# Second feed-forward layer: the output drain on VectorE alone, a longer planned transfer, an earlier planned load

## The chip, the cores and the metric

The kernel runs on one core of one Trainium2 chip. The metric is device time in microseconds for one execution, the median of several runs; a profile of one further execution is at hand. Engines are named as in the profile: PE is TensorE, PEld its weight loads, DVE is VectorE, ACT is ScalarE, POOL is GpSimd, SP is the queue that issues most DMA transfers.

## The reference

A block-causal attention over 4 sequences of 576 tokens (8 heads of 64), then two feed-forward layers on the 2304 x 512 result. The second layer, which the change touches, is this:

```python
def _moe2_ref(x, w_in, w_out, alpha):       # x 2304x512, w_in 512x2048, w_out 2048x512
    h = x @ w_in
    g = np.maximum(h, 0.0) + alpha * np.minimum(h, 0.0)
    return (g @ w_out).astype(np.float32)
```

Every operand of the second layer's matmuls is split into a high and a low fp16 part, and each product is three matmuls (high by high, high by low, low by high; helper `three`, L1030).

## The kernel before

**Tiles and steps.** The second layer works on nine tiles of 256 tokens, n = 0 to 8, and for each on eight steps s = 0 to 7 of 256 of the 2048 hidden columns. Tiles 0 and 1 run together, interleaved step by step; from tile 2 on the tiles follow one another. A step has three parts. `up2` (PE) makes h in one PSUM bank by 24 matmuls of 256 columns; its banks rotate through the tags h, h, acc, acc. `act2` applies the PReLU and splits: DVE makes u (L1199 twice, then L1203), from tile 3 on POOL adds four sums (L1211), ACT copies to the high fp16 half of g (L325, the line of the helper `act`), DVE subtracts to get the low half (L1224). `down2` (PE) multiplies g by the second weights into the tile's accumulators. For tiles 0 to 2 (`down_plain`) there are two accumulator banks of 512 columns and 12 matmuls of 512 columns per step. From tile 3 on the output block is built from seven products (Strassen's scheme, `factor`), M1 to M7 in slots 0 to 6 of the program's list, which lie in half banks of four PSUM banks with the tags e, e, s, o: 21 matmuls of 256 columns per step. PE takes them in the order of slots 0, 5 (first e bank), 3, 4 (second e bank), 2, 1 (s), 6 (o).

**The overlap of tiles.** PE runs the ups some three steps ahead of the downs. The last downs of tile n-1 stand between the first ups of tile n, and after down (n-1, step 7) PE runs up (n, step 4) and up (n, step 5) back to back before down (n, step 0). That down writes the same e banks that tile n-1 has just filled, so tile n-1's accumulators have to be drained in the time of these two ups.

**The drain.** `store_plain` (tiles 0 to 2) scales two banks of 512 columns into the SBUF tile `osb`, the first on ACT, the second on DVE (L1271). `store2` (tile 3 on) copies slot 0 on ACT into one quarter of `osb`, then DVE adds the other slots, scaled by +1 or -1 times the tile's factor, in seven instructions (L1319) that write quarter by quarter; the ACT copy's result is the operand of the first of them. Two output transfers follow.

**The next x and its scale.** `load2(n)` fetches tile n's x from DRAM into `xs` (one buffer, four transfers, L1131), takes the greatest absolute value of each partition (DVE, L1136, into `xsc`), and for n of 2 and more sends these 128 values out to DRAM and back to all partitions (`row`, then `rows`, both L317, the line of the helper `dma`), where DVE takes the greatest (L1146). A few tiny DVE instructions (L454, L1151) make the scale, and ACT and DVE split x into the fp16 pair `xh` (ACT L325, DVE L1157), which `up2` reads; `xh` has two buffers. `load2(n + 1)` is called in the loop over steps, at s = 1 of tile n.

**Who sets the order.** All instructions are first listed with a due time `plan.at`; `Plan.order` then simulates the engines with written-in costs and gives each engine one fixed order: among the instructions that are ready when the engine is free, the one with the smallest due time. On the chip each engine runs its list strictly in order. A transfer's planned cost comes from the size that is passed to `dma`; the third argument is in KiB, and `extra = kib / 350` us is added to its planned end:

```python
def dma(dst, src, kib, reads=(), writes=(), after=()):
    return add("DMA", 0.5, lambda: nc.sync.dma_start(dst(), src()), reads, writes, kib / 350.0, after)
```

The size passed does not alter the transfer. `rows` was given 64 KiB, which plans 0.18 us beyond the fixed planned part.

Of the kernel before, what the change touches and what calls it, by code (L numbers as in the profile page):

```python
# [14 lines left out]
ALU = mybir.AluOpType  # L15
# [217 lines left out]
def dve2_cost(n, pointers=0, shared=False):  # L233
    return (155 + 60 * pointers + n / 0.96) * (1.1 if shared else 1.0) * 1e-3
# [15 lines left out]
def block_causal_attention_silu_prelu(  # L250
# [65 lines left out]
    def dma(dst, src, kib, reads=(), writes=(), after=()):  # L316
        return add("DMA", 0.5, lambda: nc.sync.dma_start(dst(), src()), reads, writes, kib / 350.0, after)  # L317

    def act(n, dst, src, func, reads, writes, psum=False, **kw):
        pointers = sum(callable(kw.get(x)) for x in ("scale", "bias"))  # L320
        cost = act_cost(n, psum, pointers, "accum_out" in kw)

        def fn():
            k = {x: y() if callable(y) else y for x, y in kw.items()}
            nc.scalar.activation(dst(), src(), func, **k)  # L325

        return add("ACT", cost, fn, reads, writes)
# [799 lines left out]
    def load2(n, after=()):  # L1127
        s = sb(ff2_p, [128, T2 // 32, KD, 32], F32, "xs")
        x2 = x2d[places[n]]
        for z in range(4):  # L1130
            add("DMA", 0.5, lambda z=z: nc.sync.dma_start(  # L1131
                s()[32 * z:32 * z + 32].rearrange("p i k t -> p i (k t)"),
                x2()[:, 128 * z:128 * z + 128].rearrange("(i p) n -> p i n", p=32)),
                [x2], [(s, z)], extra=T2 / 350.0, after=after)
        sc = xsc[n] = sb(ff2_p, [128, 4], F32, "xsc", 3)
        add("DVE", dve_cost(KD * T2), lambda: nc.vector.tensor_reduce(  # L1136
            sc()[:, 0:1], s().rearrange("p i k t -> p (i k t)"), axis=AX.X, op=ALU.max, apply_absolute_value=True),
            [s], [sc])
        if n < TOGETHER2:
            spread(lambda: sc()[:, 0:1], [sc], lambda: sc()[:, 1:2], [sc])  # L1140
        else:
            row = sb(dram_p, [1, 128], F32, f"row{n}")
            rows = sb(ff2_p, [128, 128], F32, "rows")
            dma(lambda: row().rearrange("o p -> p o"), lambda: sc()[:, 0:1], 1, [sc], [row])
            dma(lambda: rows(), lambda: row().to_broadcast([128, 128]), 64, [row], [rows])
            add("DVE", dve_cost(128), lambda: nc.vector.tensor_reduce(sc()[:, 1:2], rows(), axis=AX.X, op=ALU.max),  # L1146
                [rows], [sc])
        m = lambda: sc()[:, 1:2].bitcast(I32)
        tiny(m, m, 0x7F800000, None, ALU.bitwise_and, None, sc)
        tiny(m, m, float(27 << 23), float(TOP << 23), ALU.max, ALU.subtract, sc)  # L1150
        add("DVE", dve_cost(6), lambda: nc.vector.reciprocal(sc()[:, 2:3], sc()[:, 1:2]), [sc], [sc])  # L1151
        t = sb(ff2_p, [128, 2, KD, T2], F16, "xh2", 2)
        for kk in range(KD):
            part = lambda e, kk=kk: t()[:, e, kk].rearrange("p (i t) -> p i t", t=32)
            act(T2, lambda part=part: part(0), lambda kk=kk: s()[:, :, kk], AF.Copy, [s, sc], [(t, (0, kk))],
                scale=lambda: sc()[:, 2:3])
            add("DVE", dve_cost(T2, 1, 1), lambda part=part, kk=kk: nc.vector.scalar_tensor_tensor(  # L1157
                part(1), s()[:, :, kk], sc()[:, 2:3], part(0), op0=ALU.mult, op1=ALU.subtract),
                [s, sc, (t, (0, kk))], [(t, (1, kk))])
        for kind in "io":  # L1160
            if kind in wsc:
                add("DVE", dve_cost(1, 1, 1), lambda kind=kind: nc.vector.tensor_scalar(
                    sc()[:, 1:2], sc()[:, 1:2], wsc[kind]()[:, 2:3], 2.0**(G_EXP if kind == "i" else 0),
                    op0=ALU.mult, op1=ALU.mult), [sc, wsc[kind]], [sc])
        tiny(lambda: sc()[:, 3:4], lambda: sc()[:, 1:2], -1.0, None, ALU.mult, None, sc)
        xh2[n] = t
# [99 lines left out]
    def store_plain(n):  # L1266
        sc = xsc[n]
        e = sb(ff2_p, [128, 2, DM], F32, "osb", 2)
        for t, a in enumerate(acc.pop(n)):
            if t:  # L1270
                add("DVE", dve2_cost(DM, 1), lambda a=a: nc.vector.tensor_scalar(  # L1271
                    e()[:, 1], a(), sc()[:, 1:2], None, op0=ALU.mult), [a, sc], [(e, t)])
            else:
                act(DM, lambda: e()[:, 0], lambda a=a: a(), AF.Copy, [a, sc], [(e, t)], psum=True,
                    scale=lambda: sc()[:, 1:2])
            row = 0
            for r0, count in rows_of(2 * places[n] + t):
                dma(lambda r0=r0, count=count: out[r0:r0 + count],
                    lambda row=row, count=count, t=t: e()[row:row + count, t], count * 2, [(e, t)])
                row += count  # L1280
# [18 lines left out]
    def store2(n):  # L1299
        if n < PLAIN:  # L1300
            return store_plain(n)
        sc = xsc.pop(n)
        banks = acc.pop(n)
        e = sb(ff2_p, [128, 2, DM], F32, "osb", 2)
        c11, c12, c21, c22 = ((j, half) for j in range(2) for half in range(2))
        at = lambda c: lambda: e()[:, c[0], 256 * c[1]:256 * c[1] + 256]

        def part(i):
            bank, half = SLOTS_OF[i]
            return (banks[bank], half), lambda: banks[bank]()[:, 256 * half:256 * half + 256]  # L1310

        key, m1 = part(0)
        act(256, at(c11), m1, AF.Copy, [key, sc], [(e, c11)], psum=True, scale=lambda: sc()[:, 1:2])
        for i, col, base, dst in (
            (5, 1, c11, c22), (3, 3, c22, c21), (4, 1, c22, c12), (4, 1, c21, c22), (2, 1, c11, c11), (1, 3, c21, c21),
            (6, 3, c12, c12),
        ):
            key, m = part(i)
            add("DVE", dve2_cost(256, 1), lambda m=m, col=col, base=base, dst=dst: nc.vector.scalar_tensor_tensor(  # L1319
                at(dst)(), m(), sc()[:, col:col + 1], at(base)(), op0=ALU.mult, op1=ALU.add),  # L1320
                [key, sc, (e, base)], [(e, dst)])
            for j in range(2):
                if i != {0: 6, 1: 1}[j]:
                    continue
                row = 0
                for r0, count in rows_of(2 * places[n] + 1 - j):
                    dma(lambda r0=r0, count=count: out[r0:r0 + count],
                        lambda row=row, count=count, j=j: e()[row:row + count, j], count * 2,
                        [(e, c) for c in ((c11, c12), (c21, c22))[j]])
                    row += count  # L1330
# [115 lines left out]
    for s in range(half + 1):  # L1446
        base = total + 1 + STEP_FIRST * s
        if s < half:
            for m in order2[2 * s:2 * s + 2]:
                plan.at = base - 1.0  # L1450
                load_w(1, "o", m, scanned)
                plan.at = base
                split_w(1, "o", m)
            for n in range(TOGETHER2):
                plan.at = base + 0.4 * n
                up2(n, s)
                act2(n, s)
            if s == 3:
                load2(TOGETHER2, after=stores[-2:])
        elif low_parts:  # L1460
            low_parts.pop()(())
        if s:
            for n in range(TOGETHER2):
                plan.at = base + FIRST_DOWN + 0.4 * n
                down2(n, s - 1)
    for n in range(TOGETHER2):
        store2(n)
    for k in range((N2 - TOGETHER2) * half + 1):
        n, s = divmod(k, half)
        n += TOGETHER2  # L1470
        base = after_first + STEP2 * k
        if n < N2:
            plan.at = base
            up2(n, s)
            act2(n, s)
            if n == TOGETHER2:
                plan.at = base + 1.0
                mix_o(s)
            if s == 1 and n + 1 < N2:
                load2(n + 1)  # L1480
        elif low_parts:
            low_parts.pop()(())
        if k >= 1:
            pn, s = divmod(k - 1, half)
            plan.at = base + DOWN2 + (SWITCH - 0.4 * s if s < 3 else 0.0)
            down2(pn + TOGETHER2, s)
            if s == half - 1:
                store2(pn + TOGETHER2)

    with tc.manual_schedule():  # L1490
# [86 lines left out]
```

## Time and profile before

| | |
|---|---|
| median of 3 runs | 913.66 us (913.22 to 916.06) |
| the profiled execution | 913.75 us, span 912.0 us |
| PE busy | 885.8 us, 97% of the span |
| DVE busy | 694.3 us, 76% |
| ACT busy | 465.2 us, 51% |
| POOL busy | 263.5 us, 29% |
| mean granted PE clock | 0.996 of full speed |

The span is the time from the first to the last recorded instruction. The second layer's work on PE takes the time from about 529 us to the end. An engine's busy time counts instructions alone; the end of a matmul is modelled, so consecutive matmuls overlap a little in the rows, and the time that a stretch of PE work takes is read from the start of its first matmul to the start of the next piece.

### The profile page before, as it was taken

The numbers are of one execution on the slowest core, as the hardware profiler recorded it, in microseconds if no ns is written. First come the engines' busy times: TensorE is split into PE (matmuls) and PEld (weight loads), VectorE is DVE, ScalarE is ACT, GpSimd is POOL, SyncE is SP. The second block draws the span as 40 slices with busy tenths as digits, with TensorE's granted clock in tenths as the row PEclk, the third lists the DMA queues.
The fourth block names the chain that finished last, engine by engine and source line by source line (L and its number), as shares of the span: only waits on it lengthen the run. The fifth ranks groups of instructions, "written<-read, shape, count | busy, mean of one in ns | idle before, by whom it ended". The sixth has DMA issues, their size and how long they took to land. (4 is left out here: it accounts for less than half of the span.)

```text
span 912.0 us, 18221 instructions
## 1 busy us (share of the span) xinstructions
PE 885.8 (97%) x6845; PEld 741.3 (81%) x6845; DVE 694.3 (76%) x1557; ACT 465.2 (51%) x1070; POOL 263.5 (29%) x380
## 2 busy tenths in 40 slices
PE   7899999999999999999999999999989999999997
PEld 5688888898988888889788786667658888888886
DVE  5999767688888888887489897896575856757673
ACT  6987556677868777775236753342122222213121
POOL 6501002232212222221000000572044544536552
PEclk9999999999999999999999999999999999999999
DMA  9952134487665766659698981441110110100010
GB/s 316 407 215 53 35 94 110 110 145 151 123 162 119 155 134 130 151 134 251 222 327 321 268 282 42 142 160 47 27 50 4 47 28 24 28 28 1 24 24 24
DMA packets 134248, 116.55 MB, mean 128 GB/s; under 512 B 100240, under 2 KB 111504, under 8 KB 134160
## 3 DMA queue, kind: packets, MB, share of 16 engines
q1 hardware_dynamic: 133008, 111.19, 44.4%
q0 software_dynamic: 1152, 4.19, 1.1%
q8 instruction: 54, 0.88, 0.5%
q14 instruction: 34, 0.28, 0.1%
HBM read 78.65 MB, written 14.16 MB: 102 GB/s over the span
## 5 line engine op out<-in xcount | busy, mean ns | idle before, releaser
L1030 PE MATMUL h<-x_all,w0i 128*128 128x256 f32 (+1 forms) x1440 | 224.7, 308 | 2.4 <-ACT x_all L325 1.5
L1030 PEld LDWEIGHTS h<-x_all,w0i 128*128 128x128 f32 x1440 | 199.8, 191 | 22.9 <-issue 3.8
L1030 PEld LDWEIGHTS <-w1i 128*128 128x128 f16 x1728 | 168.9, 98 | 24.7 <-issue 0.5
L325 ACT ACTIVATE g<-u 128x896 f16<-128x896 f32 (+1 forms) x72 | 60.7, 843 | 223.6 <-POOL u L1211 112.0
L1030 PEld LDWEIGHTS <-g 128*128 128x128 f16 x1296 | 127.2, 98 | 51.9 <-issue 8.5
L1030 PE MATMUL acc<-w0o,g 128*128 128x512 f32 x672 | 168.8, 394 | 0.2
L1211 POOL TENSOR_TENSOR u<-u 128x128 f32<-128x128 f32 x192 | 116.6, 628 | 162.9 <-DVE u L1203 75.6
L1030 PEld LDWEIGHTS acc<-w0o,g 128*128 128x128 f32 x672 | 122.4, 188 | 27.5 <-issue 2.5
L1030 PE MATMUL acc<-xh,w1i 128*128 128x256 f16 x864 | 100.0, 273 | 0.0
L335 POOL TENSOR_TENSOR g<-t,g 128x512 fp32r<-128x512 f32 x40 | 53.0, 1326 | 161.7 <-ACT g L325 157.7
L1030 PE MATMUL h<-xh,w1i 128*128 128x256 f16 x864 | 99.4, 273 | 0.0
L1224 DVE SCALAR_TENSOR_TENSOR g<-u,g 128x896 f16<-128x896 f32 (+1 forms) x72 | 74.1, 1030 | 12.7 <-ACT g L325 12.6
L325 ACT ACTIVATE p<-p,stat 128x512 f16<-128x512 f32 (+2 forms) x112 | 63.3, 608 | 22.0 <-issue 7.7
L1030 PE MATMUL e<-w1op,g 128*128 128x512 f16 (+1 forms) x336 | 67.6, 333 | 3.9 <-ACT osb L325 2.6
L325 ACT ACTIVATE p<-e,stat 128x256 f32<-128x256 f32 (+2 forms) x98 | 51.0, 527 | 33.2 <-DVE stat L946 22.3
L325 ACT ACTIVATE t<-h 128x512 f32<-128x512 f32 x72 | 43.0, 597 | 44.4 <-PE h L1030 37.7
L1030 PE MATMUL e<-w1om,g 128*128 128x256 f16 x432 | 56.6, 275 | 4.8 <-DVE osb L1319 4.2
L1075 DVE SCALAR_TENSOR_TENSOR t<-t,h 128x512 f32<-128x512 f32 x72 | 49.0, 680 | 13.7 <-ACT t L325 12.5
L325 ACT ACTIVATE g<-t 128x512 fp32r<-128x512 f32 x72 | 45.4, 630 | 19.5 <-DVE t L1075 19.0
L885 DVE SCALAR_TENSOR_TENSOR p<-p,stat,p 128x384 f16<-128x384 f32 (+1 forms) x64 | 48.4, 796 | 4.4 <-ACT p L325 4.1
L1030 PE MATMUL e<-w0o,g 128*128 128x512 f32 x192 | 49.4, 393 | 0.0
L416 POOL DMA_DIRECT2D kept<-wso x8 | 4.8, 602 | 136.2 <-DVE wso L371 70.3
(167 smaller groups left out, 1336.1 us busy)
## 6 DMA issues: line engine op xcount, KB each, us to landing
st<-qkv_b SPq DMA_DIRECT2D x16, 800.0 KB, 4.8
raw0i<-w_in SPq DMA_DIRECT2D x16, 512.0 KB, 9.9
raw0o<-w_out SPq DMA_DIRECT2D x16, 512.0 KB, 9.9
scano<-w_out SPq DMA_DIRECT2D x16, 512.0 KB, 6.6
raw1i<-w_in SPq DMA_DIRECT2D x16, 512.0 KB, 5.3
raw1o<-w_out SPq DMA_DIRECT2D x16, 512.0 KB, 5.9
scani<-w_in SPq DMA_DIRECT2D x13, 512.0 KB, 4.4
x<-x2e SPq DMA_DIRECT2D x18, 256.0 KB, 2.4
```

The costliest lines, as they stand in the source:

```text
L325: nc.scalar.activation(dst(), src(), func, **k)
L335: eng.tensor_tensor(lo(), src(), hi().bitcast(F32), op=ALU.subtract)
L416: add("POOL", 1.5, lambda: nc.gpsimd.dma_start(kept[s](), both().rearrange("p c n -> p (c n)")), [a, b], [kept[s]])
L885: add("DVE", dve_cost(n, 1, 1), lambda hl=hl, rr=rr, pr=pr: nc.vector.scalar_tensor_tensor(hl()[:, :, 1], pr(), rr(), hl()[:, :, 0], op0=A ...
L1030: nc.tensor.matmul(dst, lhs(a), rhs(b), start=(start and n == 0), stop=(stop and n == 2))
L1075: add("DVE", dve_cost(2 * T1), lambda: nc.vector.scalar_tensor_tensor(t(), t(), 1.0, h3(), op0=ALU.add, op1=ALU.mult), [t, h], [t])
L1211: add("POOL", pool2_cost(128, 2.5), lambda out_=out_, x=x, y=y, op=op: nc.gpsimd.tensor_tensor(u()[:, out_], u()[:, x], u()[:, y], op=op), ...
L1224: add("DVE", dve2_cost(blocks * 128, 0, True), lambda: nc.vector.scalar_tensor_tensor(side(1)(), src(), 2.0**-G_EXP, side(0)(), op0=ALU.mu ...
```

## The change

In `store_plain` and `store2` the ACT copy becomes a DVE `tensor_scalar`, so that a tile's whole drain is on DVE. The due times of the drains are set earlier (by 8.0 for tiles 0 and 1, by 5.0 for the others). The planned size of `rows` goes from 64 to 2600 KiB, which plans it to land 7.43 us after the fixed part instead of 0.18. `load2(n + 1)` is called at s = 0 instead of s = 1.

```diff
-            dma(lambda: rows(), lambda: row().to_broadcast([128, 128]), 64, [row], [rows])
+            dma(lambda: rows(), lambda: row().to_broadcast([128, 128]), 2600, [row], [rows])
...
         for t, a in enumerate(acc.pop(n)):
-            if t:
-                add("DVE", dve2_cost(DM, 1), lambda a=a: nc.vector.tensor_scalar(
-                    e()[:, 1], a(), sc()[:, 1:2], None, op0=ALU.mult), [a, sc], [(e, t)])
-            else:
-                act(DM, lambda: e()[:, 0], lambda a=a: a(), AF.Copy, [a, sc], [(e, t)], psum=True,
-                    scale=lambda: sc()[:, 1:2])
+            add("DVE", dve2_cost(DM, 1), lambda a=a, t=t: nc.vector.tensor_scalar(
+                e()[:, t], a(), sc()[:, 1:2], None, op0=ALU.mult), [a, sc], [(e, t)])
...
         key, m1 = part(0)
-        act(256, at(c11), m1, AF.Copy, [key, sc], [(e, c11)], psum=True, scale=lambda: sc()[:, 1:2])
+        add("DVE", dve2_cost(256, 1), lambda: nc.vector.tensor_scalar(
+            at(c11)(), m1(), sc()[:, 1:2], None, op0=ALU.mult), [key, sc], [(e, c11)])
...
+    plan.at -= 8.0
     for n in range(TOGETHER2):
         store2(n)
...
-            if s == 1 and n + 1 < N2:
+            if s == 0 and n + 1 < N2:
                 load2(n + 1)
...
             if s == half - 1:
+                plan.at -= 5.0
                 store2(pn + TOGETHER2)
```

On PE the order is row for row the same before and after. On DVE and ACT it moves from the point where tile 2's `rows` is read onward; all changed places lie in the second layer.

The first place is DVE at the end of tile 3, while PE is in tile 4. `g_9165` and `g_9222` are g of tile 4's steps 1 and 2; the u rows are those of step 3. Before:

```order
L1199 TENSOR_SCALAR u<-acc,alpha_sb 128x256 x2
L1203 SCALAR_TENSOR_TENSOR u<-acc,u 128x512
L1319 SCALAR_TENSOR_TENSOR osb<-e,xsc,osb 128x256
L1224 SCALAR_TENSOR_TENSOR g_9222<-u,g_9222 128x896
L1319 SCALAR_TENSOR_TENSOR osb<-e,xsc,osb 128x256 x2
L1319 SCALAR_TENSOR_TENSOR osb<-s,xsc,osb 128x256
L1319 SCALAR_TENSOR_TENSOR osb<-e,xsc,osb 128x256
L1319 SCALAR_TENSOR_TENSOR osb<-o,xsc,osb 128x256
```

And the same place in the change:

```order
L1199 TENSOR_SCALAR u<-acc,alpha_sb 128x256
L1309 TENSOR_SCALAR osb<-e,xsc 128x256
L1199 TENSOR_SCALAR u<-acc,alpha_sb 128x256
L1316 SCALAR_TENSOR_TENSOR osb<-e,xsc,osb 128x256
L1203 SCALAR_TENSOR_TENSOR u<-acc,u 128x512
L1316 SCALAR_TENSOR_TENSOR osb<-e,xsc,osb 128x256 x2
L1316 SCALAR_TENSOR_TENSOR osb<-s,xsc,osb 128x256
L1316 SCALAR_TENSOR_TENSOR osb<-e,xsc,osb 128x256
L1316 SCALAR_TENSOR_TENSOR osb<-o,xsc,osb 128x256
L1316 SCALAR_TENSOR_TENSOR osb<-s,xsc,osb 128x256
L1224 SCALAR_TENSOR_TENSOR g_9222<-u,g_9222 128x896
```

The drain has eight DVE instructions instead of seven, it begins between the two u instructions of step 3, and g of step 2 stands behind it instead of behind its first instruction.

The second place is DVE at the end of tiles 0 and 1, where tile 3's x is measured (L1136) and its scale comes back (L1146). `g_8268` and `g_8290` are g of tile 2's steps 1 and 2. Before:

```order
L1271 TENSOR_SCALAR osb<-e,xsc 128x512
L1224 SCALAR_TENSOR_TENSOR g_8268<-u,g_8268 128x512
L1136 TENSOR_REDUCE xsc<-xs 128x1
L1271 TENSOR_SCALAR osb<-o,xsc 128x512
L1199 TENSOR_SCALAR u<-acc,alpha_sb 128x256 x2
L1203 SCALAR_TENSOR_TENSOR u<-acc,u 128x512
L1224 SCALAR_TENSOR_TENSOR g_8290<-u,g_8290 128x512
L1199 TENSOR_SCALAR u<-h,alpha_sb 128x256
L1146 TENSOR_REDUCE xsc<-rows 128x1
```

The change has there (the gap holds u and g of tile 2's steps 4 and 5, three rows a step):

```order
L1270 TENSOR_SCALAR osb<-e,xsc 128x512 x2
L1224 SCALAR_TENSOR_TENSOR g_8268<-u,g_8268 128x512
L1270 TENSOR_SCALAR osb<-s,xsc 128x512
L1270 TENSOR_SCALAR osb<-o,xsc 128x512
L1136 TENSOR_REDUCE xsc<-xs 128x1
L1199 TENSOR_SCALAR u<-acc,alpha_sb 128x256 x2
L1203 SCALAR_TENSOR_TENSOR u<-acc,u 128x512
...
L1199 TENSOR_SCALAR u<-acc,alpha_sb 128x256 x2
L1203 SCALAR_TENSOR_TENSOR u<-acc,u 128x512
L1146 TENSOR_REDUCE xsc<-rows 128x1
```

All four drains stand ahead of L1136 now, and between L1136 and L1146 there are four steps' u work instead of one and a half.

The third place is SP's queue there: the transfers of tile 2's x scale are done, `x_3` and `x_4` are the x of tiles 3 and 4.

```order
 L1131 DMA xs<-x_3_3530 32x8x128 x4
-L317 DMA out<-osb 128x512 x3
-L317 DMA row_8322<-xsc 128x1
-L317 DMA out<-osb 128x512
-L317 DMA rows<-row_8322 128x128
+L317 DMA out<-osb 128x512 x4
+L317 DMA row_8344<-xsc 128x1
+L317 DMA rows<-row_8344 128x128
 L1131 DMA xs<-x_4_4538 32x8x128 x4
```

`row` stands behind four output transfers instead of three; the loads of `xs` keep their place behind the previous tile's `rows`.

## Rows read from the trace of the kernel before

**Rows 1.** PE's waits, 560 to 912 us: us in total, times, longest.

```profile
PE e L1030 <- DVE osb L1319: 4.2, 4, 1.5
PE e L1030 <- ACT osb L325: 2.6, 1, 2.6
PE e L1030 <- DVE g L1224: 1.3, 1, 1.3
PE e L1030 <- DVE osb L1271: 0.5, 1, 0.5
```

**Rows 2.** Stretches of PE work: bounds, length, busy us (instructions), granted clock, DMA.

```profile
662.31:664.90 2.59, 2.59 (x14) 1.00 0.07 23
667.52:671.58 4.06, 2.76 (x14) 1.00 0.02 5
628.43:633.67 5.24, 5.24 (x50) 1.00 0.48 155
671.58:679.63 8.05, 5.41 (x50) 1.00 0.22 65
883.52:885.81 2.29, 2.29 (x23) 1.00 0.61 140
679.63:683.94 4.31, 3.77 (x21) 0.60 0.34 122
720.95:723.84 2.89, 2.58 (x24) 1.00 0.19 72
760.84:764.78 3.94, 2.58 (x23) 1.00 0.16 56
801.79:805.43 3.64, 2.58 (x23) 1.00 0.15 56
842.44:846.51 4.07, 2.58 (x23) 1.00 0.14 51
```

**Rows 3.** PE in order of time, tile 5's first down: start, us, work [idle<-releaser].

```profile
763.02 0.81 PE L1030 MATMUL e<-w1om,g 128*128 128x256 f16 x6 [1.36 <-DVE osb L1319]
...
764.78 2.78 PE L1030 MATMUL acc<-xh,w1i 128*128 128x256 f16 x24
```

**Rows 4.** ACT in order of time, at the ends of tiles 2 and 4.

```profile
678.91 0.67 ACT L325 ACTIVATE osb<-e,xsc 128x512 f32<-128x512 f32 x1
...
759.34 0.46 ACT L325 ACTIVATE osb<-e,xsc 128x256 f32<-128x256 f32 x1
```

**Rows 5.** DVE in order of time, at the ends of tiles 2 and 4.

```profile
680.33 0.74 DVE L1271 TENSOR_SCALAR osb<-e,xsc 128x512 f32<-128x512 f32 x1
...
759.83 0.48 DVE L1319 SCALAR_TENSOR_TENSOR osb<-e,xsc,osb 128x256 f32<-128x256 f32 x1 [1.35 <-ACT osb L325]
760.23 1.17 DVE L1224 SCALAR_TENSOR_TENSOR g<-u,g 128x896 f16<-128x896 f32 x1
761.32 0.86 DVE L1319 SCALAR_TENSOR_TENSOR osb<-e,xsc,osb 128x256 f32<-128x256 f32 x2
...
762.50 0.47 DVE L1319 SCALAR_TENSOR_TENSOR osb<-e,xsc,osb 128x256 f32<-128x256 f32 x1
```

**Rows 6.** DVE's waits, whole span.

```profile
DVE xsc L1146 <- DMA rows<-row: 54.4, 7, 9.9
```

**Rows 7.** DVE in order of time, x of tiles 3 and 4.

```profile
628.07 1.21 DVE L1136 TENSOR_REDUCE xsc<-xs 128x1 f32<-128x1024 f32 x1
...
642.26 0.29 DVE L1146 TENSOR_REDUCE xsc<-rows 128x1 f32<-128x128 f32 x1 [9.62 <-DMA rows<-row]
...
645.95 1.66 DVE L1157 SCALAR_TENSOR_TENSOR xh<-xs,xsc,xh 128x256 f16<-128x256 f32 x4
...
665.46 0.29 DVE L1146 TENSOR_REDUCE xsc<-rows 128x1 f32<-128x128 f32 x1 [9.94 <-DMA rows<-row]
```

**Rows 8.** SP in order of time, tile 3's scale on its way out.

```profile
629.31 0.33 SPq L317 DMA_DIRECT2D row<-xsc  x1
```

**Rows 9.** PE in order of time, tile 3's first up.

```profile
649.27 2.78 PE L1030 MATMUL h<-xh,w1i 128*128 128x256 f16 x24
```

## The prediction

> **What bounds the kernel now.** I read the page's busy times first, as the table above has them: PE is busy for 885.8 of 912.0 us, and no other engine comes near it. A change that leaves PE's own list as it is, and this one does, can only gain where PE stands still. So the second view is PE's waits from 560 us on [rows 1]: the reader is to see that all of them are the second layer's downs into the accumulators with tag e, waiting for a drain (`osb`, on DVE or ACT) or once for a g. They sum to 8.6 us. The third view shows what they really cost: stretches of PE work from the first matmul of a piece to the first of the next, beside an undisturbed twin [rows 2]. A plain down step takes 2.59 us undisturbed, two ups 5.24, a Strassen down step 2.29. Against these:
>
> - down (tile 2, step 7): 4.06 instead of 2.59, 1.47 lost, behind a late g;
> - the two ups and the wait after them: 8.05 instead of 5.24, 2.81 lost, behind tile 2's drain on ACT;
> - down (3, 0): 4.31 instead of 2.29, 2.02 lost. Here the granted clock is 0.60, between the levels of 1.2 and 2.4 GHz, after PE had stood still for over 2.6 us; a second wait of 0.5 us for the drain on DVE is in it;
> - down (4, 0), (5, 0), (6, 0), (7, 0): 2.89, 3.94, 3.64, 4.07 instead of 2.29: 0.60 + 1.65 + 1.35 + 1.78 = 5.38 lost at the ends of tiles 3 to 6. Down (8, 0), at the end of tile 7, is the undisturbed twin itself, in the same code.
>
> Together 1.47 + 2.81 + 2.02 + 5.38 = 11.68 us, more than the 8.6 us of idle time, since the slower clock and the refilling of the pipeline come on top.
>
> The fourth view says why the drains are late: DVE stands for 54.4 us in seven waits for `rows` [rows 6], up to 9.9 us each. PE runs some three steps ahead of the downs, so it doesn't feel those waits themselves; it feels that DVE and, behind it, ACT reach the drain late. At tile 7's end, where no next x is left to wait for, PE loses nothing.
>
> **The change part by part.** *The drain from tile 3 on.* At the end of tile 4, ACT drains slot 0 at 759.34 in 0.46 us [rows 4], and by the list it stands there behind a copy of g. DVE meanwhile stands 1.35 us, drains slot 5, runs a g between, and comes to the last read of the second e bank at 762.50 for 0.47 us [rows 5]; at 763.02 PE starts into that bank, after 1.36 us of waiting [rows 3]. In the changed order neither the 1.35 us nor that g lies ahead of this read. The g takes 761.32 - 760.23 = 1.09 us from start to start. Slot 0's drain comes on top: its shape on DVE is not in the trace before; by its twins it is 0.46 us (the ACT copy) to 0.48 us (a drain with one operand more), of which 760.23 - 759.83 = 0.4 us count from start to start, since DVE instructions overlap a little. So the bank is free 1.35 + 1.09 - 0.4 = 2.0 us earlier even if DVE comes to the drain as late as now. The longest loss of the four is 1.78 us. All 5.38 us should go without any help from the rest; tile 7's end stays as it is, and so does the final drain, where slot 0 on DVE takes the place of ACT with the same duration.
>
> What stands behind the drain: g of step 2 moves behind eight instructions instead of one, 0.4 + 6 x 0.4 = 2.8 us, and saves the 1.35 us. It ends by about 763 instead of 761.4; PE reads it in down (5, 2), which follows down (5, 0), an up of 2.6 us and another down, so from 764.78 + 2.62 + 2.29 = 769.7 us on [rows 3]. Six microseconds of cover. L1136 stands behind that g, and its x is needed a tile later.
>
> *The drain of tile 2.* Now ACT drains at 678.91 for 0.67 us [rows 4], DVE at 680.33 for 0.74 us [rows 5]. With the change both are on DVE, behind tile 4's L1146, the two u rows and L1203 of step 3 and two `xh` rows. Down (2, 7) then ends at 667.52 + 2.59 = 670.1, the two ups at 675.4. L1146 comes at 665.46 now [rows 7] and at most half a microsecond later with the change (below). What stands between it and the drains is less than what stood between L1146 at 642.26 and the end of tile 3's last `xh` at 645.95 + 1.66 = 647.6, which took 5.35 us. So the drains start by 666 + 5.4 = 671.4 and end by 672.9. That leaves 2.5 us; 2.81 + 2.02 go.
>
> *The late g.* g of (2, 7) stands behind L1146 at 665.46, which had waited 9.94 us [rows 7]. In the changed order it stands two steps ahead of L1146. The 1.47 us go.
>
> *The longer plan for `rows`.* It issues the same transfers, and only their readers move: between L1136 and L1146 there are now some four steps of u and g, where there were one and a half to two. The way itself takes 642.26 - 628.07 = 14.2 us from L1136's start to L1146's [rows 7], three steps of PE at 2.62 + 2.29 = 4.9 us are about as much, so most of the 54.4 us of waiting should vanish from DVE. On PE it is worth nothing beyond what is counted.
>
> *The edit's dangerous place* is tile 3's x, the only one needed within its own tile's length. Three drains of 0.74 us or less now stand ahead of L1136 that did not, and the fourth output transfer stands ahead of `row` on SP, but it is released as the drains end, before L1136 ends. L1136 therefore starts at most 2.2 us later, at 630.3; `row`, now at 629.31 [rows 8], follows to 631.5, and L1146 to 644.5 instead of 642.26. From there to the end of the last `xh` it takes the same 5.35 us at most, with u and g of a step in between that the changed order has put elsewhere, and 0.29 + 1.66 = 1.95 us at least. So the last `xh` ends between 646.4 and 649.8; tile 3's first up starts at 649.27 [rows 9]. Cost: 0 to 0.6 us. I take 0, since the changed list has only one g and three tiny instructions left in between.
>
> *The load a step sooner.* `xs` has one buffer, so its transfers wait for the previous `xh` whatever their due time, and in SP's list they keep their place. Nothing.
>
> *Added and taken work.* DVE gets nine drains, 3 x 0.74 + 6 x 0.47 = 5.0 us in all, ACT loses as much. DVE is 76% busy and, relieved of 54.4 us of waiting, covers it.
>
> **The sum.** The profiled execution took 913.75 us, within 0.1 of the median of 913.66. 913.66 - 11.68 = **902.0 us**. If every end kept a tenth of a microsecond and tile 3's x cost its 0.6, it would be 903.2 (seven places, 0.7 us, and 0.6).
>
> **The rivals.**
>
> *The drain on one engine is no earlier.* If slot 0 waits on DVE, in order, where ACT could have taken it beside, the ends of tiles 3 to 6 keep their loss of 5.38 us; only the part around tile 2 is won, 6.30 us: 907.4. With 0.4 us more at each of five ends, 909.3. Against it: ACT's copy is not shorter than DVE's, and DVE stood idle for it. This is also where the Trainium skill speaks against the change: its page TensorEngine Tiling (Array Packing), section PSUM Bottleneck, advises to use both ScalarE and VectorE for emptying PSUM. By that rule the 909.3 would be the result; the rows show the second engine being waited for, 1.35 us for a copy of 0.46.
>
> *Tile 3's x is late*, and PE stands at its first up: by up to 3 us if the way through memory is slower behind four output transfers. 903 to 905.
>
> *The change does not do what it says*: the drain starts as late as ever for a reason that I don't see, and the waits only change their names. 911 to 914.
>
> *Slower.* Where the drains now stand ahead of g of step 2, PE could wait for that g in down (n, 2). The price: 7 instructions of 0.4 us at five ends, 14 us, and 1.5 us at tile 2's, against the 11.68 won: 917.5. It decides once that g is more than 6 us later than now, and by the order it is some 2 us later.
>
> **How the numbers follow.** A change under 0.3%, 2.7 us, can't be told from none here. Chances: forecast 0.70 (901 to 903.3), one engine no earlier 0.12 (907 to 909.3), tile 3's x late 0.07, no effect 0.06, slower 0.05. The range from 900.8 to 907.5 holds the forecast, the late x and a part of the one-engine case, some 0.8. Faster: 0.70 + 0.12 + 0.07 and the lower part of the no-effect case, 0.90; same 0.05; slower 0.05.
>
> **What would show it.** In the changed profile PE's waits for `osb` and for g after 560 us should be gone from the list, the granted clock 1.00 from 667 to 684 us, down (n, 0) 2.29 us for every n from 3 on, and two ups 5.24. L1146's wait should fall from 54.4 us to under 10, most of it at tile 3. The forecast is wrong if PE waits for `xh` near 649 us, for a g behind a drain, or for L1316 as it does for L1319 now.

## The result and the profile after

The changed kernel takes 900.5 us, the median of four runs (900.05 to 906.0), beside 913.44 us for the kernel before (four runs, 912.96 to 916.06): ratio 0.9866, 95% interval 0.9824 to 0.9909. The forecast was 902.0, with a range from 900.8 to 907.5: the time lies 0.3 us below the range.

The profiled execution took 900.05 us, span 898.2. Its busy times (page, part 1):

```profile
PE 881.2 (98%) x6845; PEld 739.8 (82%) x6845; DVE 698.2 (78%) x1566; ACT 461.4 (51%) x1061; POOL 264.0 (29%) x380
```

The list of PE's waits from 530 us to the end, which held the four lines of [rows 1], is empty. The stretches that answer to [rows 2], with the same columns: tile 2's last down, the two ups, the first down of tiles 3 to 7, and the whole neighbourhood of tile 2's end:

```profile
665.38:667.97 2.59, 2.59 (x14) 1.18 (x12) 2.38 (x6) 1.85 (x5) 0.00 (x0) 1.00 0.03 6
667.97:673.21 5.24, 5.24 (x49) 4.69 (x48) 5.24 (x12) 0.95 (x1) 1.88 (x5) 1.00 0.62 188
673.21:675.51 2.30, 2.30 (x24) 2.06 (x22) 2.19 (x4) 0.00 (x0) 2.22 (x4) 1.00 0.17 27
712.51:714.81 2.30, 2.30 (x24) 2.05 (x22) 2.16 (x5) 0.00 (x0) 0.98 (x1) 1.00 0.04 3
751.81:754.11 2.30, 2.30 (x24) 2.06 (x22) 2.16 (x5) 0.00 (x0) 0.98 (x1) 1.00 0.03 0
791.11:793.41 2.30, 2.30 (x24) 2.06 (x22) 2.16 (x5) 0.00 (x0) 0.98 (x1) 1.00 0.11 7
830.41:832.71 2.30, 2.30 (x24) 2.06 (x22) 2.16 (x5) 0.00 (x0) 1.91 (x3) 1.00 0.00 0
667.00:684.00 17.00, 17.00 (x153) 14.77 (x151) 13.33 (x23) 4.03 (x5) 9.47 (x16) 1.00 0.23 63
```

Here each row goes on, behind PE's, with the busy time of PEld, DVE, ACT and POOL; the three last columns are the granted clock, the DMA share and GB/s. Every stretch has its undisturbed length: 2.59, 5.24 and 2.30 us at a clock of 1.00.

DVE's waits in the second layer, which answer to [rows 6]:

```profile
DVE u L1199 <- PE acc L1030: 57.1, 23, 4.3
DVE u L1199 <- PE h L1030: 16.4, 14, 3.0
...
DVE xsc L1146 <- DMA rows<-row: 0.8, 2, 0.6
```

Of the 54.4 us of waiting for `rows` 0.8 are left. Instead DVE's u rows wait 73.5 us for PE, where they waited 15.9 before (11.3 + 4.6): DVE now runs ahead and stands idle because PE has not made the next h yet. PE loses nothing by it. DVE in order of time, first the x of tile 3 (as [rows 7]), then the drain of tile 2 and that of tile 4 (as [rows 5]):

```profile
625.51 1.21 DVE L1136 TENSOR_REDUCE xsc<-xs 128x1 f32<-128x1024 f32 x1
...
639.15 0.29 DVE L1146 TENSOR_REDUCE xsc<-rows 128x1 f32<-128x128 f32 x1 [0.61 <-DMA rows<-row]
...
641.11 1.68 DVE L1157 SCALAR_TENSOR_TENSOR xh<-xs,xsc,xh 128x256 f16<-128x256 f32 x4 [0.63 <-ACT xh L325]
...
667.77 1.40 DVE L1270 TENSOR_SCALAR osb<-e,xsc 128x512 f32<-128x512 f32 x2
...
745.14 0.48 DVE L1309 TENSOR_SCALAR osb<-e,xsc 128x256 f32<-128x256 f32 x1 [0.17 <-PE e L1030]
...
748.09 0.47 DVE L1316 SCALAR_TENSOR_TENSOR osb<-e,xsc,osb 128x256 f32<-128x256 f32 x1
```

And PE's first up of tile 3 (as [rows 9]):

```profile
647.13 2.78 PE L1030 MATMUL h<-xh,w1i 128*128 128x256 f16 x24
```

Tile 3's last `xh` ends at 642.79, 4.3 us ahead of its up. Tile 2's drain ends at 669.2, 4.0 us ahead of the down at 673.21. The last read of tile 4's second e bank ends at 748.56; PE comes to that bank 0.65 us after 751.81, so there are 3.9 us of room, and the same at the ends of tiles 3, 5, 6 and 7.

**A measure for the experiments.** The first layer's program is the same in all kernels here, but the first matmul that reads `xh` starts anywhere from 526.74 to 533.05 us in the profiles. So the second layer's length, from that matmul to the end of the span, is what I compare: before 912.0 - 529.06 = 382.94 us, after 898.2 - 526.74 = 371.46. That is 11.48 us won, against 11.68 in the prediction's sum. The two profiled executions differ by 13.7 us; 2.3 of them are the first layer's.

### The profile page after: what moved, and what is told of

It reads as the page before. It is cut to its first block, busy times and chain, and to the rows that moved or that the text cites. A ratio compares the mean times of both kernels' runs of the same rounds, so it can differ in the third digit from the quotient of the medians.

```text
span 898.2 us, 18229 instructions
## 1 busy us (share of the span) xinstructions
PE 881.2 (98%) x6845; PEld 739.8 (82%) x6845; DVE 698.2 (78%) x1566; ACT 461.4 (51%) x1061; POOL 264.0 (29%) x380
## 4 chain that ended last, share of the span: by engine, by line
PE 62%; DMA 4%; DVE 3%; issue 1%; ACT 1%; POOL 0%; DVEq 0%; SPq 0%; ACTq 0%
PE h L1030 19%; PE acc L1030 18%; PE e L1030 13%; PE s L1030 5%; PE o L1030 3%; DMA scani<-w_in 2%; PE e L734 2%; PE o L908 1%; DMA raw1i<-w_in 1%; PE s L734 1%; PE o L918 0%; ACT p L325 0%; DVE stat L852 0%; DVE wmaxi L469 0%; DVE t L1075 0%
## 5 line engine op out<-in xcount | busy, mean ns | idle before, releaser
L1224 DVE SCALAR_TENSOR_TENSOR g<-u,g 128x896 f16<-128x896 f32 (+1 forms) x72 | 71.7, 996 | 8.2 <-ACT g L325 8.1
L1199 DVE TENSOR_SCALAR u<-acc,alpha_sb 128x256 f32<-128x256 f32 x72 | 32.0, 478 | 57.7 <-PE acc L1030 57.1
L1075 DVE SCALAR_TENSOR_TENSOR t<-t,h 128x512 f32<-128x512 f32 x72 | 49.0, 681 | 11.7 <-ACT t L325 10.5
L325 ACT ACTIVATE g<-t 128x512 fp32r<-128x512 f32 x72 | 45.4, 631 | 21.2 <-DVE t L1075 20.6
```

The source lines that it names most:

```text
L1075: add("DVE", dve_cost(2 * T1), lambda: nc.vector.scalar_tensor_tensor(t(), t(), 1.0, h3(), op0=ALU.add, op1=ALU.mult), [t, h], [t])
L1199: add("DVE", dve2_cost(T2, 1), lambda c=c, m=m: nc.vector.tensor_scalar(u()[:, 2 * c:2 * c + 2].rearrange("p i t -> p (i t)"), h()[:, T2 * ...
L1224: add("DVE", dve2_cost(blocks * 128, 0, True), lambda: nc.vector.scalar_tensor_tensor(side(1)(), src(), 2.0**-G_EXP, side(0)(), op0=ALU.mu ...
```

## The experiments

All are told with their second layer's length and, where PE loses time, with the loss at each tile's end, worked out as in the prediction (the stretch less 2.59, 5.24 or 2.29). In diffs, "-" is the kernel named and "+" the experiment.

**e1: the long plan alone**, on the kernel before.

```diff
-            dma(lambda: rows(), lambda: row().to_broadcast([128, 128]), 64, [row], [rows])
+            dma(lambda: rows(), lambda: row().to_broadcast([128, 128]), 2600, [row], [rows])
```

> The kernel before with the planned size of rows at 2600 KiB and nothing else; slot 0 and the plain tiles' first banks are drained on ACT as before. PE's own list is row for row that of both kernels. Lateness theory (DVE reaches the drains late because it stood at L1146; moving L1146 is enough): the late g, tile 2's drain and the ends of tiles 3 to 6 all go, as tile 7's end is free in the kernel before with the same ACT copy; down (n, 0) 2.29 us for n of 4 and more, total 901 to 902.5, no PE wait for osb. Engine theory (the ACT copy in the chain is what makes the drain late): the ends of tiles 3 to 6 keep most of their 5.38 us, total 906 to 909, PE still waits for L1319. Prediction's own steps: as the lateness theory, 901.8.

Measured: 902.01 us, ratio 0.9844 (0.9809 to 0.9878); second layer 900.1 - 528.87 = 371.23. PE has no wait after 530 us, and none is left for `rows`. The whole gain is there, with the drain on ACT and DVE as before. DVE still waits for ACT's copy once, in the last drain of all (893.33 us), and the second layer is no longer for it than with that drain on DVE:

```profile
DVE osb L1319 <- ACT osb L325: 3.0, 1, 3.0
```

**e2: the drain on DVE and its earlier due times**, with 64 KiB and the load at s = 1.

```diff
-                act(DM, lambda: e()[:, 0], lambda a=a: a(), AF.Copy, [a, sc], [(e, t)], psum=True,
-                    scale=lambda: sc()[:, 1:2])
+            add("DVE", dve2_cost(DM, 1), lambda a=a, t=t: nc.vector.tensor_scalar(
+                e()[:, t], a(), sc()[:, 1:2], None, op0=ALU.mult), [a, sc], [(e, t)])
...
-        act(256, at(c11), m1, AF.Copy, [key, sc], [(e, c11)], psum=True, scale=lambda: sc()[:, 1:2])
+        add("DVE", dve2_cost(256, 1), lambda: nc.vector.tensor_scalar(
+            at(c11)(), m1(), sc()[:, 1:2], None, op0=ALU.mult), [key, sc], [(e, c11)])
...
+    plan.at -= 8.0
...
+                plan.at -= 5.0
```

> The kernel before with the whole drain on DVE and the drains' earlier due times, rows planned at 64 KiB and the load at s = 1 as before. L1146 then still stands one and a half to two steps behind L1136, so DVE still waits some 50 us there. Prediction's own steps (at the ends of tiles 3 to 6 the drain alone gives 2.0 us, more than any loss there, but the part around tile 2 needs L1146 moved): 5.38 us won, 6.3 kept, total 908.1, down (4..7, 0) 2.29 us each, and a wait near tile 2's end as before. Engine theory (who drains is what counts): tile 2's end goes too, total 901.5 to 904. Lateness theory in its strict form (only L1146's place counts): total 912 to 914, PE waits for L1316 in place of L1319.

Measured: 912.29 us, ratio 0.9968 (0.9952 to 0.9985); second layer 908.8 - 528.98 = 379.82. PE's waits, from 530 us:

```profile
PE e L1030 <- DVE osb L1270: 5.6, 1, 5.6
PE e L1030 <- DVE xsc L454: 0.7, 1, 0.7
```

The ends of tiles 3 to 6 lose nothing, though DVE still stands 57.6 us for `rows`. Tile 2's end loses 0.84 + 5.76 + 1.94 = 8.54 us in place of 6.30. DVE and, last, ACT in order of time show why:

```profile
667.11 0.29 DVE L1146 TENSOR_REDUCE xsc<-rows 128x1 f32<-128x128 f32 x1 [9.45 <-DMA rows<-row]
...
681.08 1.40 DVE L1270 TENSOR_SCALAR osb<-e,xsc 128x512 f32<-128x512 f32 x2
```

```profile
682.46 0.95 ACT L325 ACTIVATE g<-u 128x896 f16<-128x896 f32 x1 [2.72 <-POOL u L1211]
```

Both drains stand in order behind 14 us that DVE's list takes after the wait, while ACT is idle for 2.72 us, from 679.74 on. Before, ACT at least took the first one at 678.91 [rows 4]. A part of the 8.54 is that L1146 itself came late here (667.11 instead of 665.46), which e9 goes into. So the prediction's own steps (908.1) were right on the ends of tiles 3 to 6 and too low on tile 2's. The time is that of the strict lateness theory, but not its mechanism: no wait for L1316 is left.

**e3: the drain back on ACT, the rest of the change kept**, and **e4: the load back at s = 1, the rest kept.**

```diff
-        add("DVE", dve2_cost(256, 1), lambda: nc.vector.tensor_scalar(
-            at(c11)(), m1(), sc()[:, 1:2], None, op0=ALU.mult), [key, sc], [(e, c11)])
+        act(256, at(c11), m1, AF.Copy, [key, sc], [(e, c11)], psum=True, scale=lambda: sc()[:, 1:2])
```

```diff
-            if s == 0 and n + 1 < N2:
+            if s == 1 and n + 1 < N2:
```

(e3 does the same in `store_plain`.)

> The changed kernel with the two drains given back to ACT; long plan, earlier load and earlier due times stay. If the drain's engine gives nothing once L1146 is moved, the time is that of the changed kernel, 900 to 902, with no PE wait for osb. If the drain on DVE gives the 5.38 us at the ends of tiles 3 to 6, 905.5 to 907.

> The changed kernel with the load called at s = 1 again. On PE, ACT, SP and POOL the order is row for row that of the changed kernel; on DVE a few tiny rows trade places. All theories: 900 to 901.5, L1136 and the xs transfers at the same places to 0.5 us, since xs waits for its one buffer.

Measured: e3 903.04 us, second layer 901.1 - 529.8 = 371.3; e4 901.71 us, second layer 899.9 - 528.67 = 371.23. Neither has a wait on PE after 530 us. With the long plan it makes no difference to PE which engine drains, or when the load is called; that the executions took up to 903.04 us, above what was expected, is the first layer's doing (it ends at 529.8 and 528.67 us, and at 526.74 in the changed kernel's profile).

**e5 and e6: slot 0's drain issued 9 and 17 times** for tiles 3 to 7, in the changed kernel; the extra ones write the same values.

```diff
-            at(c11)(), m1(), sc()[:, 1:2], None, op0=ALU.mult), [key, sc], [(e, c11)])
+            at(c11)(), m1(), sc()[:, 1:2], None, op0=ALU.mult) for _ in range(9 if n < N2 - 1 else 1)],
+            [key, sc], [(e, c11)])
```

> The changed kernel, with the first drain instruction of tiles 3 to 7 (slot 0, L1309) issued nine times in place of once; the eight more write the same values again. From start to start such a drain takes 0.39 us, so the second e bank is read out 8 x 0.39 = 3.1 us later. In the changed kernel's trace it is read out at 748.56 us at the end of tile 4, and PE comes to it at 752.46: 3.9 us of room, and the same at all five ends. Theory (PE feels a drain only past that room): no loss, second layer 371.5 us, execution 900 to 902 us. Rival (DVE is now the engine whose work PE follows, since PE's waits were won by freeing DVE): every added microsecond shows, 5 x 3.1 = 15.7 us, execution near 916.

> The same with slot 0's drain issued seventeen times: 16 x 0.39 = 6.2 us later at each of five ends, 2.3 us more than the room of 3.9 us. Theory: PE waits 2.3 us at each end, 11.7 us in all if nothing comes on top, second layer 383 us, execution 912 to 916 with what the clock may add. Rival (each added microsecond shows): 31 us, execution near 931.

Measured: e5 908.26 us, second layer 906.5 - 533.05 = 373.45; e6 934.82 us, second layer 933.0 - 528.19 = 404.8. The execution times missed both theories; e5's because its first layer is the longest of all. DVE in e5, then PE at the end of the same tile 4:

```profile
751.71 4.64 DVE L1309 TENSOR_SCALAR osb<-e,xsc 128x256 f32<-128x256 f32 x9 [0.17 <-PE e L1030]
756.27 0.47 DVE L1199 TENSOR_SCALAR u<-acc,alpha_sb 128x256 f32<-128x256 f32 x1
```

```profile
758.39 0.49 PE L1030 MATMUL e<-w1op,g 128*128 128x256 f16 x3
758.71 1.45 PE L1030 MATMUL e<-w1om,g 128*128 128x256 f16 x9
```

A repeated drain of one quarter takes 0.51 us from start to start (756.27 - 751.71 = 4.56 for nine), not the 0.39 that I took from drains of different quarters. So e5 adds 4.56 - 0.40 = 4.2 us (0.40 being one such drain) against a room of 3.9. PE then loses 0.44 us at each end (here the 1.45 instead of 1.15 us, and the row after it), 2.2 in all: the room is real, and of some 21 us of added DVE work PE feels a tenth. That refutes the rival by which every microsecond on DVE shows. In e6 the seventeen add 762.03 - 753.32 - 0.40 = 8.3 us, 4.4 more than the room. DVE, PE, and PE's clock at the end of tile 4:

```profile
753.32 8.79 DVE L1309 TENSOR_SCALAR osb<-e,xsc 128x256 f32<-128x256 f32 x17 [0.17 <-PE e L1030]
762.03 0.47 DVE L1199 TENSOR_SCALAR u<-acc,alpha_sb 128x256 f32<-128x256 f32 x1
```

```profile
762.95 0.49 PE L1030 MATMUL e<-w1op,g 128*128 128x256 f16 x3 [2.79 <-DVE osb L1317]
...
765.11 1.44 PE L1030 MATMUL e<-w1om,g 128*128 128x256 f16 x6 [1.35 <-DVE osb L1317]
```

```profile
762.95:768.26 5.31, 3.96 (x21) 2.81 (x21) 5.31 (x10) 0.95 (x1) 1.74 (x4) 0.68 0.28 102
```

The idle time is 2.79 + 1.35 = 4.14 us, near what the room says. But the second layer is 33.3 us longer, 6.7 at each of five ends: some 2.5 us an end come on top, while the granted clock falls to 0.68, between 1.2 and 2.4 GHz. The theory had the place right and the price too low. That 33.3 us lie near the rival's 31 bears nothing out: the rival's 31 was for 6.2 us added at each end, and with the 8.3 that were added it would be 41; the idle time at each end is half of what was added.

**e7 and e11: the plan at 700 and 1300 KiB** in the kernel before, to see how much of the longer plan is needed (the diff is that of e1 with another number).

> The kernel before, with the planned size of the transfer to rows at 700 KiB in place of 2600. In its order two steps' u stand between L1136 and L1146 for the x of tiles 2 to 5 and three for tiles 6 to 8 (before: 2, 1, 1, 2, 2, 2, 2; with 2600: 4, 3, 3, 3, 4, 4, 4). Theory (a tile's end is freed as soon as the L1146 that stands ahead of its drain is one step of PE, 4.9 us, later): tile 2's end goes free, for L1146 of tile 4's x has one step more; so do the ends of tiles 4 to 6; the end of tile 3, behind L1146 of tile 5's x with its two steps as before, keeps its 0.60 us. Second layer 371.4 + 0.6 = 372.0 us, execution 901 to 904, though DVE still waits some 54.4 - 5 x 4.9 = 30 us for rows. Rival (PE's loss goes with DVE's wait for rows): 30 of 54.4 us of wait left, so 6.4 of the 11.7 us of loss stay: second layer 378 us, execution 908.

> The kernel before with the planned size of rows at 1300 KiB. In its order the x of tile 4 still has two steps' u between L1136 and L1146, as with 700, all others have three; with 700 the x of tile 5 had two as well, and the ends of tiles 2 and 3 kept 2.07 and 0.97 us. Theory (each end hangs on the L1146 ahead of its own drain, one step more frees it): tile 3's end goes free, tile 2's keeps 1.5 to 2.5 us, second layer 373 to 374 us. Rival (what is left is the total of DVE's waits for rows): some 25 of 54.4 us of waiting left, a loss spread over all the ends, 374 to 376 us.

Measured: e7 907.03 us, second layer 905.1 - 530.85 = 374.25; e11 903.41 us, second layer 901.3 - 528.66 = 372.64. PE's waits in e7, then in e11:

```profile
PE e L1030 <- ACT osb L325: 1.0, 1, 1.0
PE e L1030 <- DVE osb L1271: 0.7, 1, 0.7
PE e L1030 <- DVE osb L1319: 0.7, 1, 0.7
```

```profile
PE e L1030 <- DVE osb L1271: 0.7, 1, 0.7
PE e L1030 <- ACT osb L325: 0.4, 1, 0.4
```

| planned KiB | DVE's wait for `rows`, us | lost at the end of tile 2 | tile 3 | tiles 4 to 6 |
|---|---|---|---|---|
| 64 (before) | 54.4 | 6.30 | 0.60 | 4.78 |
| 700 (e7) | 40.6 | 2.07 | 0.97 | 0 |
| 1300 (e11) | 34.3 | 1.38 | 0 | 0 |
| 2600 (e1) | 0 | 0 | 0 | 0 |

The theory was right on the ends of tiles 3 to 6: with one step more between L1136 and L1146 of the x whose L1146 stands ahead of the drain, the end goes free; tile 3's, with its two steps unchanged at 700, does not. It was wrong on tile 2's end in e7, which one step more did not free (374.25 us instead of 372.0); what keeps it there was not followed. In e11 it was a little off: 372.64 and 1.38 us, just under the 373 to 374 and 1.5 to 2.5 expected. The rival fails in both: three quarters of PE's loss (8.6 of 11.7) go with a quarter of the wait (13.8 of 54.4).

**e8: the drain of tiles 3 to 8 alone on DVE**, with the earlier due time for them, and **e10: the same without the due time**, both on the kernel before, where tile 2's drain stays.

```diff
-        act(256, at(c11), m1, AF.Copy, [key, sc], [(e, c11)], psum=True, scale=lambda: sc()[:, 1:2])
+        add("DVE", dve2_cost(256, 1), lambda: nc.vector.tensor_scalar(
+            at(c11)(), m1(), sc()[:, 1:2], None, op0=ALU.mult), [key, sc], [(e, c11)])
...
+                if pn + TOGETHER2 >= PLAIN:
+                    plan.at -= 5.0
```

(The last two lines are e8's.)

> The kernel before, with the drain on DVE and due 5.0 earlier for tiles 3 to 8 alone; tile 2's drain, the planned size of 64 KiB and the load stay as before. The prediction's claim by itself: all 5.38 us at the ends of tiles 3 to 6 go without help from the rest, and tile 2's end keeps its 6.30: second layer 377.6 us, ratio 0.994, 908. Rival (with the long plan gone, DVE comes to the drain as late as before and the ends keep part of the loss, so that what the drain and plan give is one gain counted once): 910 to 912, with waits for L1316 at down (4, 0) to (7, 0).

> The kernel before with the drain of tiles 3 to 8 on DVE, and nothing else; the due times stay too. In its order g of step 2 stays between the drain's DVE instructions, as before. By the prediction's step only the wait for ACT of 1.35 us less the drain of 0.4 us goes, 0.95 us an end, and the g of 1.09 us stays ahead of the second e bank: of 0.60 + 1.65 + 1.35 + 1.78 us at the ends of tiles 3 to 6 there stay 0 + 0.7 + 0.4 + 0.83, some 1.9 us, with waits for L1319's successor L1316; with tile 2's end the second layer is 379.5 to 381 us. Rival (the engine alone decides, not the place of g): nothing stays at those ends, as with the earlier due times: 377.6 to 379.

Measured: e8 909.85 us, ratio 0.9942 (0.992 to 0.9963), second layer 907.8 - 528.69 = 379.1; e10 909.82 us, second layer 908.0 - 527.74 = 380.26. PE's waits in e8, then in e10:

```profile
PE e L1030 <- DVE g L1224: 3.6, 1, 3.6
PE e L1030 <- ACT osb L325: 1.0, 1, 1.0
PE e L1030 <- DVE osb L1271: 0.7, 1, 0.7
```

```profile
PE e L1030 <- DVE g L1224: 4.3, 1, 4.3
PE e L1030 <- DVE osb L1271: 0.7, 1, 0.7
PE e L1030 <- DVE osb L1320: 0.6, 1, 0.6
```

In e8 nothing is lost at the ends of tiles 3 to 6: the 5.38 us go by the drain and its due time alone, as the prediction claimed. In e10 tile 3's end keeps 0.90 us and the others keep nothing. So the total of 380.26 lies where I expected it, but not for my reason. That does not show that the engine alone decides, for the planner also rearranged the lists ahead of these ends: on ACT, for one, an `xh` copy at 741.11 us now stands ahead of a g that it stood behind. DVE at the end of tile 4, before and then in e10:

```profile
756.88 0.88 DVE L1199 TENSOR_SCALAR u<-acc,alpha_sb 128x256 f32<-128x256 f32 x2
```

```profile
756.51 0.88 DVE L1199 TENSOR_SCALAR u<-acc,alpha_sb 128x256 f32<-128x256 f32 x2
...
761.44 0.47 DVE L1320 SCALAR_TENSOR_TENSOR osb<-e,xsc,osb 128x256 f32<-128x256 f32 x1
```

DVE begins step 3's u 5.16 us ahead of the down at 761.67, before 3.96 us ahead of the one at 760.84: 1.20 us are won by the list. From there to the end of the last read of the second e bank it takes 5.40 us instead of 6.09 (to 762.97 [rows 5]): 0.69 us are won by the engine, with the g still in between, where I expected 0.95. Together they turn 1.48 us too late into 0.41 us too early. At tile 3's end the engine gives 0.68 us as well, but there DVE begins that u 0.99 us later before the down than in the kernel before, and PE waits.

At tile 2's end e8 loses 7.47 us and e10 8.15, with DVE's order the same as before ahead of it (6.30 before). DVE in the kernel before, then in e8:

```profile
652.19 1.22 DVE L1136 TENSOR_REDUCE xsc<-xs 128x1 f32<-128x1024 f32 x1 [1.44 <-DMA xs<-x]
```

```profile
654.34 1.22 DVE L1136 TENSOR_REDUCE xsc<-xs 128x1 f32<-128x1024 f32 x1 [3.01 <-DMA xs<-x]
...
667.79 0.28 DVE L1146 TENSOR_REDUCE xsc<-rows 128x1 f32<-128x128 f32 x1 [10.12 <-DMA rows<-row]
```

L1136 of tile 4's x came 2.15 us later than before: its load was issued 0.6 us later on SP (648.22, and 647.64 before) and took 1.6 us longer, 6.1 us from there to L1136 instead of 4.5. So L1146 came later too (667.79, and 665.46 in [rows 7]), and the g behind it.

**e9: the kernel before once more.**

> The kernel before, unchanged, once more, for a second profile. Theory (what PE loses at the end of tile 2 hangs on when the x of tile 4 comes through memory, which differs from execution to execution; the order is fixed): the ends of tiles 3 to 6 lose 0.6 to 1.8 us each as in the first profile, and the end of tile 2 something from 5 to 8 us; the first layer may end anywhere from 526 to 533 us. Rival (the first profile is what this program always does): second layer 382.9 us within 0.2, and 6.30 us lost at the end of tile 2.

Measured: 914.1 us, second layer 912.3 - 529.38 = 382.92. Its waits on PE:

```profile
PE e L1030 <- DVE osb L1319: 3.7, 3, 1.7
PE e L1030 <- ACT osb L325: 2.6, 1, 2.6
PE e L1030 <- DVE g L1224: 1.4, 1, 1.4
PE e L1030 <- DVE osb L1271: 0.7, 1, 0.7
```

The second layer has the same length within 0.02 us, as the rival had it, but not the same losses: 6.69 us at tile 2's end, and 0.31, 1.95, 1.55 and 1.09 at the ends of tiles 3 to 6 (0.60, 1.65, 1.35 and 1.78 before; the theory's 0.6 to 1.8 held at two of the four). Tile 2's end, in four executions whose order is the same up to there, goes with how far L1146 of tile 4's x comes ahead of the last down's start: 2.1 us ahead in the first profile, 6.30 lost; 2.0 ahead in e9, 6.69; 0.3 behind in e8, 7.47; 1.0 behind in e10, 8.15. That this differs from execution to execution, as the theory had it, is not shown: the two executions of the kernel before agree, and tile 4's load takes 4.55 and 4.53 us in them; the longer ones (5.4 us in e2, 6.1 in e8, 5.9 in e10) are in other kernels, and what makes them longer was not tried.

## Why the prediction was right, point by point

The losses that it named were the right ones, and so was their sum. Where it went wrong is which part of the change buys them; as all parts were made at once, the total could not show that.

**What bounds the kernel.** Right. Each of PE's waits after 560 us went, and with them 11.48 us of the second layer against 11.68 in the sum. The stretches read beside their undisturbed twins gave the right size where the waits alone (8.6 us) would have been 2.9 short.

**The drain from tile 3 on.** The claim that the 5.38 us go without help from the rest holds (e8, e2). Its working, 1.35 + 1.09 - 0.4 = 2.0 us, holds in size too. In e8, at the end of tile 4, DVE shows the first u of step 3 and the last read of the second e bank:

```profile
757.45 0.48 DVE L1199 TENSOR_SCALAR u<-acc,alpha_sb 128x256 f32<-128x256 f32 x1
...
760.80 0.48 DVE L1320 SCALAR_TENSOR_TENSOR osb<-e,xsc,osb 128x256 f32<-128x256 f32 x1
```

From the one's start to the other's end it takes 3.83 us, before 6.09: 2.26 us won, and DVE came to that u no earlier (3.94 us ahead of the down at 761.39, before 3.96). Of this the engine alone gives 0.69 (e10); the rest goes with the g and the drain's earlier place.

**Tile 2's drain.** It ended 4.0 us ahead of need where 2.5 were predicted. The prediction rested it on DVE's list at that end, and that list is what the long plan makes. With the drain moved and the plan left short (e2), the same two instructions came at 681.08, and nothing was saved at that end. So the 2.81 + 2.02 us belong to the plan, not to the drain's move.

**The longer plan.** Here the attribution failed, though not the time: "on PE it is worth nothing beyond what is counted". The plan by itself is worth all that is counted (e1: 371.23 us), since a DVE that does not stand for `rows` reaches the drain early, and then ACT's copy is early too. At tiles 3 to 6 the drain's move and the plan each suffice, so the parts do not add: with the drain's move alone 7.47 and 8.54 us remain, all at tile 2's end (e8, e2), with the plan alone nothing. With the drain on ACT, what decides is not how long DVE waits in all (e7 and e11 leave 40.6 and 34.3 us of waiting and lose 3.04 and 1.38) but whether DVE gets through the work behind the wait that stands ahead of a drain in time.

**Tile 3's x**, the dangerous place: the last `xh` ends 4.3 us before its up, where I expected 2.9 us before to 0.5 us after it. L1136 did not start 2.2 us later; measured from tile 3's first up it starts 0.4 us sooner (21.6 us ahead instead of 21.2). The drains ahead of it had themselves moved up.

**The load a step sooner** is worth nothing, as predicted (e4). **The late g** went, as predicted.

**The rivals.** One engine draining is no later, and with the long plan two engines are no better: the Trainium skill's rule to empty PSUM with both (TensorEngine Tiling (Array Packing), section PSUM Bottleneck) brings no gain here, 371.3 us with both (e3) against 371.46 with one. In e2 there may be a case for two engines: at tile 2's end, behind a DVE that is late, the drains began only at 681.08, while ACT stood idle from 679.74. What that is worth was not measured: e2 lost 8.54 us there, e8 and e10, with ACT and L1146 later still, 7.47 and 8.15, but their due times differ from e2's too. The late g that would make it slower had its room.

**The measured time** is 1.5 us under the forecast, and the second layer explains none of that: it won 0.2 us less than the sum. In the profiled pair the first layer is 2.3 us shorter after, of which the prediction has nothing; with a second layer of the same length e1, e3 and e4 took 901.71 to 903.04 us. The prediction took the first layer as fixed, and on the scale of a microsecond or two it is not; the last section has what differs there.

## What to carry to other kernels

When a wait on an in-order engine is followed by work that another engine needs, first move the wait later in the list: telling the planner how long the transfer really takes (the way back took 14.2 us from L1136 to L1146 [rows 7], and the plan had room for some two steps of 4.9 us) won all 11.5 us by one number. Take the parts of a change one by one before crediting them: two of these freed the same ends, and one of them alone left the largest loss, at another end, in place. Measure room by adding work (e5, e6): it tells how far an engine is from the path, where busy shares of 76% and 78% tell nothing.

## What the runs showed of the hardware

**A wait costs more than its length, and a long one much more.** PE's waits of 0.8 to 1.66 us at the ends of tiles 4 to 6 (before and e9) left the granted clock at 1.00, and each cost 0.29 us beyond its length (1.95 lost for a wait of 1.66). After 2.63 us of waiting the clock was 0.64 in e9, after 3.65 us 0.56 in e8, after 5.59 us 0.52 in e2, between the levels of 1.2 and 2.4 GHz; after 2.79 us, with 1.05 to 1.35 more behind, it fell to 0.54 to 0.72 at all five ends in e6, for some 2.5 us of extra time each.

```profile
680.04:684.70 4.66, 3.97 (x21) 2.74 (x21) 4.53 (x7) 0.95 (x1) 2.62 (x5) 0.64 0.31 113
761.37:765.61 4.24, 2.58 (x23) 2.04 (x21) 4.24 (x10) 0.89 (x1) 0.00 (x0) 1.00 0.15 52
```

(Stretches of e9, the first downs of tiles 3 and 5; columns as above.)

**The same program's first layer does not take the same time.** In the profiles its end differs by 6.3 us. In five of the thirteen (both of the kernel before, e5, e7 and e8; not the changed kernel's) the granted clock between 440 and 460 us was 0.91, in the others 1.00. PE's waits differ too: e5, whose first layer is the longest, has one of 1.8 us for POOL's p and one of 1.1 us for `x_all` that the first profile of the kernel before does not have. What sets them off was not tried.

**A drain instruction repeated on the same quarter** took 0.51 us from start to start on DVE (4.56 us for nine in e5), drains of one quarter after another 0.39 to 0.40 (745.14 to 745.54 in the changed kernel). The repeats read and write the same places; what makes the difference was not tried.
